# A gate stage in written order on four engines, with the rows of w_sp asked for two pairs ahead

## The chip, the cores and the metric

The kernel runs on one core of a Trainium2 chip. The time is the device time of one execution in microseconds; lower is better. Five engines work side by side, each through its own list of instructions in order: PE (matrix products, with PEld as its weight loads), ACT, DVE, POOL, and SP, which here only issues transfers. They wait for each other through semaphores. PE writes to PSUM, of which this stage uses four banks for its products; SBUF holds everything else.

## What is computed

One transformer block on x of 2048 x 512 in float32: attention with 32 heads, then a gated MLP whose gate mixes the rows of the sequence.

```python
h = x + _A_ref(_layernorm(x), A_wqkv, A_wo)           # attention, 32 heads of 16
z = _gelu(jnp.einsum("bsd,df->bsf", _layernorm(h), w_in))   # f = 1376
z1 = z[..., :Fh]                                      # Fh = 688
z2 = _layernorm(z[..., Fh:], axis=-1)
g = jnp.einsum("ts,bsf->btf", w_sp, z2) + b_sp[None, :, None]   # w_sp: 2048 x 2048
h2 = h + jnp.einsum("bsf,fd->bsd", z1 * g, w_out)
```

The change touches the product with `w_sp` and what follows it.

## The kernel before

The program has four parts: projections and attention; a stage that makes `z` (16 blocks of 128 rows); the gate stage; and a second pass that finishes the gate and multiplies by `w_out`. Every product is done as three products of float32r halves (`mm3`, lines 87 to 89: high x high, high x low, low x high), so an operand is first split: ACT copies the high half (L741, or L79 from PSUM), DVE subtracts it to get the low half (L742, or L84). `parts` and `split` do this, and `put` splits the two halves of a 128 x 1024 row of `w_sp` into a slot.

The product `w_sp @ z2` is 2 x 2 blocks times 2 x 2 blocks, done with seven block products in place of eight. A is `w_sp` (rows t and columns s, each in two halves), B is `z2` (s and f in two halves of 1024 and 344). The rows of A go in eight **pairs** p: rows p and p+8, in blocks of 128. For a pair, S1 = A21+A22, S2 = S1-A11, S3 = A11-A21, S4 = A12-S2. The B side (T1, T2, T3, N4) is made once, in the z stage.

- The **gate stage** (the loop at the head of the last `with`) computes for each pair g7 = S3 T3, g6 = S2 T2, g4 = A22 N4 and g5 = S1 T1, each of 8 blocks and 24 matmuls, and leaves three sums in `g_scr`: `p6` is a copy of g6 by ACT (L924), `p67` = g7+p6 (L925), `keep` adds these to g4 and g5 (L888) and stores them. S2 is stored in `s_scr`. While PE works on pair p, the operands of pair p+1 are loaded, combined and split: `rows_of_a` loads A11, A21 and A22 (six transfers of 256 KB, L747), forms S3, S1 and S2 on DVE (L761) and stores S2 (L776). Its tiles have the tags `xr` (three halves), `rc` and `o` (two halves each), so a tile of pair p+2 can be asked for only when the split of pair p+1 has read it. The split operands lie in seven slots that rotate (`old`, `now`, `new`). The products write to a pool of four banks, `ps_g`.
- Beside the last pair (`last`), the first needs of the second pass are made: A11, S4 and A12 of pair 0, the blocks of B (`b11`, one block per pair; `b22` and `b21`, eight blocks each, in the place of T3 and T2), read back from `z_scr` by `load_b` (L865) through two times three buffers, and `w_out` (`raw_u`, split to `wu`).
- The **second pass** computes for each pair g1 = A11 B11, g3 = S4 B22 and g2 = A12 B21, adds the stored sums (L1037, L1050, L1067) and the bias (L1038), multiplies by z1 (L1039 for the lower row of the pair, L1051 and L1068 for the upper), transposes (L1001), splits the transposes (`Out.turn`, L79 and L84), multiplies by `w_out` (`Out.multiply`) and adds h (`Out.store`, L1018). `fetch(p+1)` issues the loads for the next pair.

Order. In the second pass PE, ACT and DVE run in the order in which the code is written (`tc.manual_schedule`); SP there, and all engines in the gate stage, are ordered by a scheduler that has a model of each instruction's time and takes what it holds to be ready. Every engine then executes its list strictly in order. The pool tiles carry the waits: a tile is handed on when the last reader of its former content is done.

Of the kernel before, what the change touches and what calls it, by code (L numbers as in the profile page):

```python
# [18 lines left out]
P = 128  # L19
S = 2048  # L20
D = 512
# [23 lines left out]
def block_kernel(ctx: ExitStack, tc: tile.TileContext, x, wqkv, wo, w_in, w_sp4, b_sp, w_out, out):  # L45
# [717 lines left out]
    def rows_of_a(p, e):  # L763

        half = lambda name, tag: e2.tile([P, QB, P], F32, name=name, tag=tag, bufs=3 if tag == "xr" else 2)
        a11, a21, a22 = ([half(f"a{n}", tag) for _ in range(2)]
                         for n, tag in ((11, "xr"), (21, "rc"), (22, "o")))
        s3 = [e2.tile([P, QB, P], F32, name="s3", tag=f"o2{n}", bufs=1) for n in range(2)]
        load_a(a11, 0, 0, p)
        load_a(a21, 1, 0, p)  # L770
        load_a(a22, 1, 1, p)
        combine(e, s3, a11, a21, ALU.subtract)
        combine(e, a21, a21, a22, ALU.add)
        combine(e, a11, a21, a11, ALU.subtract)
        for n in range(2):
            nc.sync.dma_start(cut(s_scr[p])[n], a11[n])  # L776
        return {"s3": s3, "s2": a11, "a22": a22, "s1": a21}

    with ExitStack() as mid:
# [57 lines left out]
        for k in range(NB):  # L837
# [8 lines left out]
            if k == NB - 2:  # L846
                raw = rows_of_a(0, nc.vector)
                ops = {n: put(w[i], raw[n]) for i, n in enumerate(("s3", "s2", "a22"))}
# [3 lines left out]
    with ExitStack() as fin:  # L852
# [26 lines left out]
        ops["s1"] = put(f[0], raw["s1"])  # L879
        old, now = [None, None, f[1], f[2]], w + f[:1]  # L880
        for p in range(HB):
            nxt, new, last = {}, [old[2], old[3], now[0], now[1]], p + 1 == HB
            g7, g6, g4, g5 = [ps_g.tile([P, 512], F32, name="g")[:, :FC] for _ in range(4)]
# [7 lines left out]
            if not last:  # L891
                raw = rows_of_a(p + 1, nc.vector)
                nxt["s3"] = put(new[0], raw["s3"])
                nxt["s2"] = put(new[1], raw["s2"])
            else:
                t = [e2.tile([P, QB, P], F32, name="a11", tag="rc") for _ in range(2)]
                load_a(t, 0, 0, 0)
                a11 = put(f[0], t)
            put_b(b11, p, load_b(0, 0, p))
            if last:  # L900
                bs = [load_b(1, 1, k) for k in range(6)]

                raw_u = wc.tile([P, 4, D], F32, name="wr", tag="w2")
# [203 lines left out]
```

## Time and profile before

| | |
|---|---|
| times of three runs | 1907.54, 1910.86, 1911.50 us; median 1910.86 us |
| profiled execution | 1914.12 us; span of the core 1912.3 us, mean granted clock 0.994 |
| busy | PE 1883.8 us, DVE 1535.9, ACT 1328.8, POOL 203.9 |
| gate stage, pairs 0 to 7 | 1593.24 to 1713.80 us |
| pair 0 of the second pass | to 1749.73 us |
| pairs 1 to 7 and the end | to 1912.3 us |

How to read it: times are microseconds from the span's start. PE's busy time is counted from records whose ends are modelled, so what matters are PE's waits and its granted clock. A row of a timeline gives the start, the busy time of the (merged) instructions, engine, line, operation, output and input by the program's names with the buffer numbers left out, the shape and the count; in brackets the idle time just before and what ended it. Lines such as L742 belong to helpers that many places call; the names tell which. The line numbers are those of the kernel before.

### The profile page before, as it was taken

How to read it: one execution, taken by the hardware profiler on the slowest of the kernel's cores; microseconds unless marked ns; L12 is line 12 of the kernel's file. 1: busy time of each engine (PE TensorE's matmuls, PEld its weight loads, DVE VectorE, ACT ScalarE, POOL GpSimd, SP SyncE). 2: the span in 40 equal slices, each digit the busy share in tenths (PEclk: the TensorE clock that was granted, in tenths of full speed). 3: DMA queues.
4: the chain of work that ended last, by engine and by line, in shares of the span. 5: the costliest groups of instructions: out<-in, count | busy, mean ns of one | idle time of the engine just before them, and what ended most of it. 6: DMA issues, size and time to landing. Idle time of an engine off the chain costs nothing. (4 is left out here: it accounts for less than half of the span.)

```text
span 1912.3 us, 32432 instructions
## 1 busy us (share of the span) xinstructions
PE 1883.8 (99%) x11608; PEld 1068.5 (56%) x11608; DVE 1535.9 (80%) x3105; ACT 1328.8 (69%) x1733; POOL 203.9 (11%) x281
## 2 busy tenths in 40 slices
PE   9999999999999999999999999999999999997999
PEld 6765444444444444444444444444359989996887
DVE  6487999999999999999999999999537677665554
ACT  3335888888888888888888888888964345342221
POOL 2130000001011000000000000000015551001211
PEclk9999999999999999999999999999999999998999
DMA  5677111211221111111021021000045556657551
GB/s 189 183 199 182 40 24 31 71 25 28 49 51 32 38 34 21 37 39 24 19 50 33 13 49 31 22 13 5 7 107 161 154 172 203 191 185 237 181 180 34
DMA packets 148105, 159.82 MB, mean 84 GB/s; under 512 B 62952, under 2 KB 92664, under 8 KB 146408
## 3 DMA queue, kind: packets, MB, share of 16 engines
q1 hardware_dynamic: 143304, 146.48, 28.6%
q10 hardware_dynamic: 4608, 11.27, 1.5%
q8 instruction: 91, 1.49, 0.3%
q14 instruction: 70, 0.57, 0.1%
q0 software_dynamic: 32, 0.01, 0.0%
HBM read 101.16 MB, written 55.61 MB: 82 GB/s over the span
## 5 line engine op out<-in xcount | busy, mean ns | idle before, releaser
L611 ACT ACTIVATE pt<-s 128x1024 f32<-128x1024 f32 x1024 | 993.3, 1030 | 143.9 <-PE s L608 141.6
L208 DVE TENSOR_REDUCE mx<-m 128x1 f32<-128x512 f32 x1511 | 958.5, 683 | 104.9 <-PE m L203 61.6
L203 PE MATMUL m<-kst,qst 48*128 48x512 f32 x1511 | 606.3, 447 | 0.0
L619 PE MATMUL pv<-pt,vst 128*32 128x512 f32 x4096 | 550.9, 605 | 0.4 <-ACT o L626 0.4
L608 PE MATMUL s<-qst,kst 50*128 50x512 f32 x2048 | 465.6, 428 | 2.5 <-ACT pt L611 2.0
L203 PEld LDWEIGHTS m<-kst,qst 48*128 48x128 f32 x1511 | 262.9, 184 | 315.6 <-DVE mx L208 222.5
L608 PEld LDWEIGHTS s<-qst,kst 50*128 50x128 f32 x2048 | 222.8, 185 | 57.1 <-ACT pt L611 32.4
L203 PE MATMUL m<-uvs,qst 48*128 48x512 f32 x503 | 248.5, 495 | 0.0
L203 PEld LDWEIGHTS m<-uvs,qst 48*128 48x128 f32 x503 | 91.8, 183 | 207.2 <-DVE mx L208 205.3
L217 DVE CUSTOM_DVE_ANT_0 ab<-m,ab 128x512 f32<-128x512 f32 x252 | 171.5, 681 | 3.8 <-ACT ab L213 2.0
L619 PEld LDWEIGHTS pv<-pt,vst 128*32 128x32 f32 x4096 | 82.9, 108 | 161.0 <-issue 154.9
L213 ACT ACTIVATE ab<-m 128x512 f32<-128x512 f32 x251 | 151.2, 602 | 16.7 <-PE tp L203 10.5
L81 POOL CAST mparts<-nm 128x16 fp32r<-128x16 f32 x32 | 6.3, 196 | 910.9 <-DVE nm L223 910.9
L741 ACT ACTIVATE ws<-a 128x512 fp32r<-128x512 f32 x80 | 46.6, 624 | 66.0 <-issue 26.7
L87 PE MATMUL acc<-wi,hT 128*128 128x344 f32 x256 | 82.9, 324 | 0.0
L88 PE MATMUL acc<-wi,hT 128*128 128x344 f32 x256 | 81.8, 319 | 0.0
L89 PE MATMUL acc<-wi,hT 128*128 128x344 f32 x256 | 81.8, 319 | 0.0
L742 DVE TENSOR_TENSOR ws<-a,ws 128x512 fp32r<-128x512 f32 x80 | 56.0, 743 | 19.5 <-ACT ws L741 19.5
L87 PE MATMUL g<-b,ws 128*128 128x344 f32 x192 | 65.7, 342 | 2.7 <-ACT p L924 2.7
L79 ACT ACTIVATE pT<-tp 128x384 fp32r<-128x384 f32 (+2 forms) x48 | 18.3, 382 | 66.7 <-PE tp L1001 49.2
L88 PE MATMUL g<-b,ws 128*128 128x344 f32 x192 | 62.5, 326 | 0.0
L89 PE MATMUL g<-b,ws 128*128 128x344 f32 x192 | 62.4, 325 | 0.0
(188 smaller groups left out, 2176.4 us busy)
## 6 DMA issues: line engine op xcount, KB each, us to landing
a<-in_w_sp SPq DMA_DIRECT2D x80, 256.0 KB
qst<-q_scr SPq DMA_DIRECT2D x192, 64.0 KB
kst<-k_scr SPq DMA_DIRECT2D x48, 256.0 KB
z_scr<-z ACTq DMA_DIRECT2D x32, 344.0 KB
k_scr<-part SPq DMA_DIRECT2D x16, 512.0 KB
q_scr<-part SPq DMA_DIRECT2D x16, 512.0 KB
z<-z_scr SPq DMA_DIRECT2D x14, 344.0 KB
b<-z_scr SPq DMA_DIRECT2D x24, 172.0 KB
```

Of the source, the lines that this page charges most:

```text
L87: nc.tensor.matmul(ps, lh, rh, start=first, stop=False)
L88: nc.tensor.matmul(ps, lh, rl, start=False, stop=False)
L89: nc.tensor.matmul(ps, ll, rh, start=False, stop=last)
L203: nc.tensor.matmul(acc, q[r, p, c], keys[r, p], start=True, stop=True)
L208: nc.vector.reduce_max(at(t, e if t else e - 1), acc, axis=AX.X)
L213: nc.scalar.activation(ab[0], acc, AF.Abs)
L217: nc.vector.tensor_tensor_reduce(ab[0], acc, ab[0], 0.5, LOW, ALU.add, ALU.max, at(0, 0))
L608: nc.tensor.matmul(s[:, t, :], k[r, p, kb * P:(kb + 1) * P], q[r, p, :], start=True, stop=True)
L611: nc.scalar.activation(t, s, AF.Exp, scale=DH ** -0.5)
L619: nc.tensor.matmul(pv[0][32 * j:32 * j + 32, :], vst[hg % 2][:, c:c + 32], pts[j % 2][:, j // 2, :], start=kb == 0, stop=kb == NB - 1)
L741: nc.scalar.activation(hi, src, AF.Copy)
L742: (nc.gpsimd if el == "pool" else nc.vector).tensor_sub(lo, src, hi.bitcast(F32))
```

## The change

The arithmetic stays. The gate stage is put into `manual_schedule` for PE, ACT, DVE and SP, and the second pass is now inside the same block, so that SP runs in written order there too. `rows_of_a` is taken apart into `ask` (loads), `difference` (S3) and `sums` (S1, S2 and the store of S2), and the loads for pair p+2 are written into pair p, each behind the split that frees its buffers: A22 and A11 behind A22's split, A21 behind S1's. Within a pair S3 is now split before the sums, and `b` is asked one pair ahead. The copy `p6` stands in the code behind the split of the next pair's A22, as it did before.

In pair 6 the places of the loads that no longer have a pair are taken by A12, S2 and A11 of the second pass's pair 0 and by six blocks of `b22`; in pair 7 every split of a block asks for the next one (`put_next`). `w_out` is asked behind the last blocks of `b22`, and all its splits stand after the last `keep`. The first load of stored sums is asked behind the second `keep`. In the second pass `fetch` asks A11, S2 and A12 first, `h` is asked for the present pair, and in pair 0 the splits for pair 1 stand behind the transposes and, for A11, ahead of the first multiplication.

```diff
@@ -760,21 +760,27 @@
-    def rows_of_a(p, e):
-        half = lambda name, tag: e2.tile([P, QB, P], F32, name=name, tag=tag, bufs=3 if tag == "xr" else 2)
-        a11, a21, a22 = ([half(f"a{n}", tag) for _ in range(2)]
-                         for n, tag in ((11, "xr"), (21, "rc"), (22, "o")))
+    def half(name, tag, bufs=2):
+        return [e2.tile([P, QB, P], F32, name=name, tag=tag, bufs=bufs) for _ in range(2)]
+    def ask(i, j, p, tag):
+        t = half(f"a{i}{j}", tag, 3 if tag == "xr" else 2)
+        load_a(t, i, j, p)
+        return t
+    def difference(a11, a21):
         s3 = [e2.tile([P, QB, P], F32, name="s3", tag=f"o2{n}", bufs=1) for n in range(2)]
-        load_a(a11, 0, 0, p)
-        load_a(a21, 1, 0, p)
-        load_a(a22, 1, 1, p)
-        combine(e, s3, a11, a21, ALU.subtract)
-        combine(e, a21, a21, a22, ALU.add)
-        combine(e, a11, a21, a11, ALU.subtract)
+        combine(nc.vector, s3, a11, a21, ALU.subtract)
+        return s3
+    def sums(p, a11, a21, a22):
+        combine(nc.vector, a21, a21, a22, ALU.add)
+        combine(nc.vector, a11, a21, a11, ALU.subtract)
         for n in range(2):
             nc.sync.dma_start(cut(s_scr[p])[n], a11[n])
-        return {"s3": s3, "s2": a11, "a22": a22, "s1": a21}
@@ -844,8 +850,10 @@
             if k == NB - 2:
-                raw = rows_of_a(0, nc.vector)
-                ops = {n: put(w[i], raw[n]) for i, n in enumerate(("s3", "s2", "a22"))}
+                a11, a21, a22 = ask(0, 0, 0, "xr"), ask(1, 0, 0, "rc"), ask(1, 1, 0, "o")
+                s3 = difference(a11, a21)
+                sums(0, a11, a21, a22)
+                ops = {n: put(w[i], t) for i, (n, t) in enumerate((("s3", s3), ("s2", a11), ("a22", a22)))}
     early.close()
@@ -860,10 +868,13 @@
         def load_b(i, j, k):
-            t = (f1.tile([P, FC], F32, name="b", bufs=3) if k % 2 else
+            staged[0] += 1
+            t = (f1.tile([P, FC], F32, name="b", bufs=3) if staged[0] % 2 else
                  e2.tile([P, FC], F32, name="b", tag="hn", bufs=3))
             nc.sync.dma_start(t, z_scr[1][(HB * i + k) * P:(HB * i + k + 1) * P, j * FC:(j + 1) * FC])
             return t
+        staged = [0]
@@ -876,10 +887,14 @@
         f = [Slot(fs, f"f{i}") for i in range(3)]
-        ops["s1"] = put(f[0], raw["s1"])
+        ops["s1"] = put(f[0], a21)
         old, now = [None, None, f[1], f[2]], w + f[:1]
+        order = fin.enter_context(tc.manual_schedule(engines={E.PE, E.Activation, E.DVE, E.SP}))
+        a11, a21, a22 = ask(0, 0, 1, "xr"), ask(1, 0, 1, "rc"), ask(1, 1, 1, "o")
+        b = load_b(0, 0, 0)
         for p in range(HB):
             nxt, new, last = {}, [old[2], old[3], now[0], now[1]], p + 1 == HB
+            ahead = p + 2 if p + 2 < HB else None
             g7, g6, g4, g5 = [ps_g.tile([P, 512], F32, name="g")[:, :FC] for _ in range(4)]
@@ -889,20 +904,12 @@
             if not last:
-                raw = rows_of_a(p + 1, nc.vector)
-                nxt["s3"] = put(new[0], raw["s3"])
-                nxt["s2"] = put(new[1], raw["s2"])
+                nxt["s3"] = put(new[0], difference(a11, a21))
+                sums(p + 1, a11, a21, a22)
+                nxt["s2"] = put(new[1], a11)
             else:
-                t = [e2.tile([P, QB, P], F32, name="a11", tag="rc") for _ in range(2)]
-                load_a(t, 0, 0, 0)
-                a11 = put(f[0], t)
-            put_b(b11, p, load_b(0, 0, p))
-            if last:
-                bs = [load_b(1, 1, k) for k in range(6)]
-                raw_u = wc.tile([P, 4, D], F32, name="wr", tag="w2")
-                nc.sync.dma_start(raw_u, w_out[:4 * P, :].rearrange("(a p) c -> p a c", p=P))
-                raw_u = [raw_u[:, :2, :], raw_u[:, 2:, :]]
+                a11 = put(f[0], a11)
+            put_b(b11, p, b)
             if p:
                 product(g7, ops["s3"], T["t3"])
             else:
@@ -910,80 +917,107 @@
                     product(g7, ops["s3"], T["t3"], blocks)
                     product(g6, ops["s2"], T["t2"], blocks)
             if not last:
-                nxt["a22"] = put(new[2], raw["a22"])
+                nxt["a22"] = put(new[2], a22)
+                a22 = ask(1, 1, ahead, "o") if ahead else ask(0, 1, 0, "o")
+                if ahead:
+                    s2, a11 = a11, ask(0, 0, ahead, "xr")
+                else:
+                    s2 = half("s4", "xr", 3)
+                    for n in range(2):
+                        nc.sync.dma_start(s2[n], cut(s_scr[0])[n])
             else:
                 b22 = [zc.tile([P, HB, FC], F32R, name="b22", tag=f"t3_{i}") for i in range(2)]
-                for k in range(HB):
-                    put_b(b22, k, bs[k] if k < len(bs) else load_b(1, 1, k))
-                s4raw = [e2.tile([P, QB, P], F32, name="s4", tag="xr", bufs=3) for _ in range(2)]
-                for n in range(2):
-                    nc.sync.dma_start(s4raw[n], cut(s_scr[0])[n])
+                b21 = []
+                asked = [(1, 1, k) for k in range(6, HB)] + [(1, 0, k) for k in range(HB)]
+                def put_next(b, k):
+                    put_b(b, k, bs.pop(0))
+                    if asked:
+                        bs.append(load_b(*asked.pop(0)))
+                for k in range(6):
+                    put_next(b22, k)
+                combine(nc.vector, s2, a22, s2, ALU.subtract)
+                s4 = put(f[1], s2)
+                for k in range(6, HB):
+                    put_next(b22, k)
+                raw_u = wc.tile([P, 4, D], F32, name="wr", tag="w2")
+                nc.sync.dma_start(raw_u, w_out[:4 * P, :].rearrange("(a p) c -> p a c", p=P))
+                raw_u = [raw_u[:, :2, :], raw_u[:, 2:, :]]
             if p:
                 product(g6, ops["s2"], T["t2"])
             nc.scalar.activation(p6, g6, AF.Copy)
             nc.vector.tensor_add(p67, g7, p6)
             if not last:
-                nxt["s1"] = put(new[3], raw["s1"])
+                nxt["s1"] = put(new[3], a21)
+                if ahead:
+                    a21 = ask(1, 0, ahead, "rc")
+                else:
+                    a11 = ask(0, 0, 0, "rc")
+                b = load_b(0, 0, p + 1)
+                if not ahead:
+                    bs = [load_b(1, 1, k) for k in range(6)]
             else:
-                t = [e2.tile([P, QB, P], F32, name="a12", tag="o") for _ in range(2)]
-                load_a(t, 0, 1, 0)
-                combine(nc.vector, s4raw, t, s4raw, ALU.subtract)
-                s4 = put(f[1], s4raw)
-                a12 = put(f[2], t)
+                a12 = put(f[2], a22)
                 b21 = [zc.tile([P, HB, FC], F32R, name="b21", tag=f"t2_{i}") for i in range(2)]
                 for k in range(HB):
-                    put_b(b21, k, load_b(1, 0, k))
-            product(g4, ops["a22"], T["n4"])
-            keep(1, g4, p67)
-            if last:
+                    put_next(b21, k)
                 for f0, n in FB[4:]:
                     t = e2.tile([P, D], F32, name="wr", tag="rc")
                     nc.sync.dma_start(t[:n], w_out[f0:f0 + n, :])
                     raw_u.append(t[:n])
-                parts(wu[0][:, :2, :], wu[1][:, :2, :], raw_u[0])
+            product(g4, ops["a22"], T["n4"])
+            keep(1, g4, p67)
             product(g5, ops["s1"], T["t1"])
             keep(2, g5, p67)
+            if last:
+                t = zc.tile([P, HB * FC], F32, name="qz", tag="t1_1")
+                first = (t[:, :3 * FC].rearrange("p (i c) -> p i c", c=FC),
+                         [t[:, (3 + 2 * i) * FC:(5 + 2 * i) * FC] for i in range(2)])
+                nc.sync.dma_start(first[0], g_scr[0].rearrange("i p c -> p i c"))
             keep(0, g5, p6)
             ops, old, now = nxt, now, new
+        for i in (1, 0):
+            nc.sync.dma_start(first[1][i], z_scr[0][HB * i * P:(HB * i + 1) * P, :])
...
+        for i, places in enumerate([[w[:, 2 * i:2 * i + 2, :] for w in wu] for i in range(2)]
+                                   + [[w[:, 4, :] for w in wu], [t[:fn, j * D:(j + 1) * D] for j in range(2)]]):
+            parts(*places, raw_u[i])
...
+        rows = lambda p, i: slice((p + HB * i) * P, (p + HB * i + 1) * P)
         def fetch(p):
-            q, z1 = first if not p else (f2.tile([P, 3, FC], F32, name="q"),
...
+            raw = [half("a11"), half("a12"), half("s2")]
+            load_a(raw[0], 0, 0, p)
+            for n in range(2):
+                nc.sync.dma_start(raw[2][n], cut(s_scr[p])[n])
+            load_a(raw[1], 0, 1, p)
+            z1 = [f2.tile([P, FH], F32, name=f"z1{i}") for i in range(2)]
+            q = f2.tile([P, 3, FC], F32, name="q")
             nc.sync.dma_start(q, g_scr[p].rearrange("i p c -> p i c"))
             for i in (1, 0):
-                nc.sync.dma_start(z1[i], z_scr[0][rows[i], :])
-            raw = None
-            if p:
-                raw = [half("a11"), half("a12"), half("s2")]
-                load_a(raw[0], 0, 0, p)
-                load_a(raw[1], 0, 1, p)
-                for n in range(2):
-                    nc.sync.dma_start(raw[2][n], cut(s_scr[p])[n])
+                nc.sync.dma_start(z1[i], z_scr[0][rows(p, i), :])
+            return q, raw, z1
+        def fetch_h(p):
             h = [f2.tile([P, D], F32, name=f"h{i}") for i in range(2)]
             for i in (1, 0):
-                nc.sync.dma_start(h[i], h_scr[rows[i], :])
-            return q, raw, z1, h
+                nc.sync.dma_start(h[i], h_scr[rows(p, i), :])
+            return h
@@ -1018,63 +1052,67 @@
-        prev, nxt = None, fetch(0)
-        with tc.manual_schedule(engines={E.PE, E.Activation, E.DVE}):
-            for p in range(HB):
-                (q, _, z1, h), last = nxt, p + 1 == HB
-                nxt = None if last else fetch(p + 1)
...
+        prev, nxt = None, (first[0], None, first[1])
+        for p in range(HB):
+            (q, _, z1), last = nxt, p + 1 == HB
+            nxt = None if last else fetch(p + 1)
+            h = fetch_h(p)
...
+            if p and not last:
+                a11 = put(f[0], nxt[1][0])
...
+            if p and not last:
+                combine(nc.vector, nxt[1][2], nxt[1][1], nxt[1][2], ALU.subtract)
+                s4 = put(f[1], nxt[1][2])
...
+            if not p:
+                a11 = put(f[0], nxt[1][0])
+                bot.multiply(range(len(FB)))
+            nc.vector.tensor_add(left, g2, left)
+            (nc.vector if last else nc.gpsimd).tensor_mul(left, left, z1[0][:, :FC])
+            if not p:
+                combine(nc.vector, nxt[1][2], nxt[1][1], nxt[1][2], ALU.subtract)
+                s4 = put(f[1], nxt[1][2])
+            if not last:
+                a12 = put(f[2], nxt[1][1])
```

More of the change, by code (lines that the diff above doesn't have):

```diff
@@ L959, in block_kernel @@
-        t = zc.tile([P, HB * FC], F32, name="qz", tag="t1_1")
-        first = (t[:, :3 * FC].rearrange("p (i c) -> p i c", c=FC),
-                 [t[:, (3 + 2 * i) * FC:(5 + 2 * i) * FC] for i in range(2)])
         late.close()
         f2 = fin.enter_context(tc.tile_pool(name="fin_2", bufs=2))
+        rows = lambda p, i: slice((p + HB * i) * P, (p + HB * i + 1) * P)
         def fetch(p):
-            rows = [slice((p + HB * i) * P, (p + HB * i + 1) * P) for i in range(2)]
             half = lambda n: [f2.tile([P, QB, P], F32, name=n) for _ in range(2)]
-            q, z1 = first if not p else (f2.tile([P, 3, FC], F32, name="q"),
-                                         [f2.tile([P, FH], F32, name=f"z1{i}") for i in range(2)])
+            raw = [half("a11"), half("a12"), half("s2")]
[5 more added lines that the diff above has]
+            q = f2.tile([P, 3, FC], F32, name="q")
@@ L1081 @@
+        prev.multiply(range(3, 6), False)
+        prev.turn((0, 3))
+        prev.multiply(range(3))
+        prev.store()
 def kernel(**inputs):
```

97 lines of the change are left out of this document (39 added, 58 removed).

## The prediction

> **What bounds the kernel now.** I read the page first, then busy time by stretches, the timeline of each engine around the two seams of the gate stage, and the queue of SP. The page gives the span and shows one dip:
>
> ```profile
> span 1912.3 us, 32432 instructions
> ...
> PE   9999999999999999999999999999999999997999
> ...
> PEclk9999999999999999999999999999999999998999
> ```
>
> PE is the bound almost everywhere; only slice 37 (1721 to 1769 us) has both an idle PE and a reduced clock. Cutting the end of the program at product boundaries shows how much (length, then busy us and count for PE, PEld, DVE, ACT, POOL, then clock, DMA share, GB/s):
>
> ```profile
> 1608.37:1623.40 15.03, 15.03 (x98) 15.03 (x97) 12.41 (x23) 5.33 (x10) 0.00 (x0) 1.00 0.73 225
> 1668.60:1683.60 15.00, 15.00 (x98) 14.94 (x97) 9.89 (x18) 4.96 (x9) 0.00 (x0) 1.00 0.51 170
> 1713.80:1749.73 35.93, 22.30 (x99) 19.50 (x97) 20.97 (x37) 13.27 (x27) 2.81 (x2) 0.76 0.80 267
> 1773.50:1795.28 21.78, 21.78 (x123) 19.00 (x121) 12.50 (x22) 6.19 (x13) 4.47 (x3) 1.00 0.58 178
> ```
>
> A pair of the gate stage and a pair of the second pass are pure PE time (15.03 and 21.78 us, clock 1.00). The stretch between them, pair 0 of the second pass, takes 35.93 us at a clock of 0.76. PE's timeline there has three waits:
>
> ```profile
> 1710.04 0.32 PE L87 MATMUL g<-t,ws 128*128 128x344 f32 x1
> 1716.68 0.53 PE L87 MATMUL g<-b,ws 128*128 128x344 f32 x1 [2.71 <-ACT p L924]
> 1729.92 0.98 PE L1001 MATMUL tp<-ident,pr 128*128 128x128 f32 x6 [2.01 <-ACT pr L1038]
> 1743.11 0.80 PE L87 MATMUL acc<-wu,pT 128*128 128x512 f32 x1 [8.90 <-ACT pT L79]
> 1749.73 0.43 PE L87 MATMUL g<-b,ws 128*128 128x344 f32 x1
> ```
>
> Why they exist is on ACT, which works strictly in its order:
>
> ```profile
> 1715.79 0.49 ACT L741 ACTIVATE b<-b 128x344 fp32r<-128x344 f32 x1 [5.24 <-DMA b<-z_scr]
> 1716.18 0.44 ACT L924 ACTIVATE p<-g 128x344 f32<-128x344 f32 x1
> ...
> 1737.43 1.24 ACT L741 ACTIVATE ws<-a 128x512 fp32r<-128x512 f32 x2 [7.82 <-DMA a<-in_w_sp]
> ```
>
> The copy that frees PE a PSUM bank (L924) stood behind a split of `b` whose load had not landed, and the split of the transposes (L79) stood behind the split of `a11` for the next pair, whose load landed at 1737.4. The middle wait is named ACT, but the DVE product L1039 (start 1728.94, 0.88 us) ended at 1729.82, just before.
>
> After each wait the clock halves for a while (us stretches of 2):
>
> ```profile
> 1716.00:1718.00 2.00, 1.32 (x5) 1.32 (x6) 1.48 (x4) 2.00 (x6) 0.00 (x0) 0.71 0.48 156
> 1718.00:1720.00 2.00, 2.00 (x9) 2.00 (x8) 2.00 (x5) 2.00 (x7) 0.00 (x0) 0.50 0.55 158
> 1720.00:1722.00 2.00, 2.00 (x14) 2.00 (x13) 2.00 (x6) 2.00 (x3) 0.00 (x0) 0.94 0.57 175
> ```
>
> **The change, part by part.** *Counts.* Written out, the changed kernel has the same number of instructions on every engine, the same number of DMAs, and PE's sequence is the same instruction by instruction. So nothing is added or removed; only orders on ACT, DVE and SP change.
>
> *The seam to the second pass: removed waits.* Without waits, pair 0 of the second pass needs 72 matmuls of the gate kind at 15.03/96 = 0.157 us (11.28), six transposes (1751.72 to 1752.30, 0.58) and 18 multiplications (1754.27 to 1758.74, 4.47): 16.33 us. It took 35.93, so 19.6 us are there to win: 13.62 of waits and 5.98 of half clock. The new order takes each cause away. The 24 `b` blocks are asked from pair 6 on in a chain of six buffers, and p6 stands on ACT behind b22 alone; `a11` of pair 1 is put after the splits of pair 0's transposes. What is late next, counted on DVE from pair 7's start T with the pitches of the rows (0.605 for 128x512, 0.43 for 128x344): two keeps, a11, b11 to T+2.5; b22 must wait for g7's end (T+3.76, it takes T3's place); six of b22, the S4 combine, its split with one hop over ACT, two more, p67, a12, eight of b21 to T+15.4; three keeps to 16.7; the four splits of w_out (1.14, 1.14, 0.6, 0.6) to 20.2; three L1037 (1.5) and L1039 (0.88) to 22.6. PE reaches the transposes at T+15.03+60x0.157 = T+24.4. Slack 1.8 us, from which the last two b21, queued on SP behind the 1 MB of w_out, may take up to 1.5. The q load follows the second keep's store on SP (T+16.5); before, it was asked at 1722.18 and used at 1727.44, so at most 5.3 us: T+21.8, against 20.2 at which DVE asks for it; that too eats the slack, not more. The a11 of pair 1 is asked when the w_out splits free the memory (T+20.2); before, 1729.79 to 1737.43, 7.6 us: T+27.9, split by T+30, needed at T+31.4. I cost the seam at 0 (bounds 0 and 5: one wait of up to 3 and its clock).
>
> *The first seam: a new wait.* ps_g has four banks. Pair 1's g7 needs one of pair 0's back, and the first free one is g6's, freed by the copy p6. Before, the scheduler put p6 of pair 0 early:
>
> ```profile
> 1602.08 0.43 ACT L924 ACTIVATE p<-g 128x344 f32<-128x344 f32 x1
> ...
> 1603.52 0.69 DVE L761 TENSOR_TENSOR s<-a,a 128x512 f32<-128x512 f32 x1 [0.80 <-DMA a<-in_w_sp]
> 1604.40 0.69 DVE L761 TENSOR_TENSOR s<-a,a 128x512 f32<-128x512 f32 x1 [0.19 <-DMA a<-in_w_sp]
> 1605.01 2.49 DVE L761 TENSOR_TENSOR a<-a,a 128x512 f32<-128x512 f32 x4
> 1607.41 1.29 DVE L742 TENSOR_TENSOR ws<-s,ws 128x512 fp32r<-128x512 f32 x2
> ```
>
> In written order p6 of pair 0 stands on ACT behind all splits of pair 1's S3, S2, b and A22, and these wait for pair 1's a21, whose buffer only comes free after S1 of pair 0 (asked 1599.84, landed 1603.5 and 1604.4). Then: differences to 1605.0, S3's lower halves to 1606.3, four sums to 1608.7, then on ACT S2's second half 0.52, b 0.41, A22 2x0.52, p6 0.43: 1611.1. PE wants the bank at 1608.37, where it began without a wait before. So 2.7 us of waiting. Bounds: 2 (if the loads land half a microsecond earlier) and 4.5 (a22 is now queued behind a21: 0.5 MB more at the 213 to 325 GB/s of that stretch). The clock: the waits of 2.71 and 2.01 us were followed by 11.23 us for 60 matmuls worth 9.4, and by 4.29 us for work worth 2.45: 1.83 us each. The new wait is as long, so I add 1.8. The Trainium skill (TensorE: Matmul & The Clock Gate, Part 1) says that the array goes to half clock after at least one idle window of about 3.4 us; by that a wait of 2.7 us would keep the clock, and the sum would be -16.9. The trace does not agree: 2.01 us of idle were enough.
>
> *The steady gate pairs: 0.* DVE's own loop is: differences, splits, sums, splits to S1 (14 of 0.605, two of 0.43, a hop: 9.6 us), then the a21 load; from S1 done to the next difference it took 4.2 to 5.5 us before (1655.4 to 1659.62, 1669.5 to 1675.03), with all six loads issued in a bunch. Now a22 and a11 go out some 2 us ahead of a21, so I take 4.2: 13.8, under 15.03, and the loop keeps up. In pair 1 it starts late: from the sums (1608.7) S2, b, A22, p67 and S1 bring DVE to 1613.4, the next a21 lands at 1617.6, p6 of pair 1 comes 7.5 later at 1625.1, and g7 of pair 2 wants its bank at 1627.9 (1611.1, 15.03 and 1.8 of clock). Slack 2.8 us, growing by about 1 a pair. The cover is gone if a load takes 2.8 us longer.
>
> *SP in written order.* Behind each ask stand the stores of s_scr and q. The waiting asks are those whose buffer DVE frees late; nobody waits soon for the stores (q has two buffers). In the second pass pair p+1's loads go out some 3 us before pair p starts, its h a little later; PE has no wait there now and gets none: 0.
>
> *Sum.* -19.6 + 2.7 + 1.8 = -15.1 us. The profiled execution took 1914.12 us (span 1912.3 and 1.8 around it): it would be 1899.0. It lies 3.3 above the median of the three runs, 1910.86; from that I forecast 1895.8.
>
> **Rivals.**
> A second wait stays (at the pass-2 transposes, at pair 1's a11, or at g7 of pair 2): the slacks of 0.2 to 2.8 us are thin, and loads behind w_out took 5.24 us of ACT's time before. Price 1 to 3 us and 1.8 of clock: 1898.6 to 1900.6, two of them 1904.
> The new wait costs less: the clock stays up through an idle stretch as short as 2.7 us (the row after 2.01 us is against it), 1910.86-19.6+2.7 = 1894.0, or the loads land early enough that no wait is left, 1891.3. The Trainium skill's section named above states the first.
> Slower: the w_sp loads land late in every gate pair. Before, a late load only delayed DVE, because the scheduler put p6 ahead of the splits that wait for it; now p6 stands behind A22's split and holds a bank. If a21 lands L after its ask, DVE's loop takes 9.6+L; over 5.4 each microsecond of L makes each pair longer, and each wait adds 1.8 of clock. With L = 8 (nearest row: the 7.6 to 1737.43, in a stretch with a DMA share of 0.80, where gate pairs have 0.51 to 0.73) the first pair eats the slack and five lose 2.6+1.8, 22 us: 1917.8. It decides at L of about 7, where four to five pairs lose 3.4. The 4.2 to 5.5 of the gate pairs speak against it.
> No change to be measured: the second pass's loads only move later on SP, so that the waits at the transposes and at a11 come back whole (2.0+1.8 and 8.9+2.2): -0.2, 1910.7. Against it: pass 2's first blocks are all asked before pair 7 ends.
>
> **How the numbers follow.** Forecast (one new wait at pair 1, clean second seam) 0.50, its own range 1894.5 to 1898.5; second wait 0.22; cheaper 0.12; no change 0.06; slower 0.10. Leaving out the last two and the outer edge gives 1890.5 to 1904. A measurement tells about 0.2% (3.8 us) here from no change: faster 0.84 (the first three), same 0.06, slower 0.10.
>
> **What would show it.** Right: PE's timeline has one wait near 1608.4 of 2 to 4.5 us released by ACT's copy p<-g, then 15.03 a pair; the stretch from g5 of pair 7 to pair 1 of the second pass is 16 to 18 us at clock near 1; DVE's first L1037-like step comes before PE reaches the transposes. Wrong: no wait at pair 1 (then the bank came from elsewhere), waits of PE on ACT's p<-g in several pairs (the slower rival), or a wait at pT that names a11's load again.

## The result, and the profile after

The changed kernel took 1915.36 us (median of 8) beside 1911.18 us of the kernel before (median of 8): a ratio of 1.0023, 95% interval [1.0012, 1.0034]. In a second comparison it took 1911.98 beside 1909.79 us: 1.0009 [1.0001, 1.0018]. It is slower by one or two tenths of a per cent; the forecast was 1895.8 us.

The page of its profiled execution (1915.18 us) still has the dip in slice 37, now at 8 tenths of PE where it was 7:

```profile
span 1913.1 us, 32433 instructions
...
PE   9999999999999999999999999999999999998999
...
PEclk9999999999999999999999999999999999998999
```

Busy time by stretches, first the gate stage, then pair 0 of the second pass, called the seam below (length, then busy us and count of PE, PEld, DVE, ACT, POOL, clock, DMA share, GB/s):

```profile
1595.86:1721.47 125.61, 122.04 (x768) 120.26 (x768) 86.12 (x152) 44.91 (x86) 0.00 (x0) 1.00 0.57 184
1721.47:1750.58 29.11, 19.38 (x99) 17.13 (x97) 20.31 (x37) 13.06 (x27) 2.22 (x2) 0.82 0.80 267
```

The gate stage was 120.56 us before and is 125.6; the seam was 35.93 and is 29.1, where 16.3 was forecast. From pair 1 of the second pass on nothing changed (158.4 us from the start of its first product to that of the last in both). PE's timeline shows where the two stretches lose time:

```profile
1612.81 0.43 PE L87 MATMUL g<-t,ws 128*128 128x344 f32 x1 [1.65 <-ACT p L952]
...
1643.90 0.43 PE L87 MATMUL g<-t,ws 128*128 128x344 f32 x1 [0.48 <-ACT p L952]
1659.93 0.42 PE L87 MATMUL g<-t,ws 128*128 128x344 f32 x1 [0.70 <-ACT p L952]
...
1706.33 0.42 PE L87 MATMUL g<-t,ws 128*128 128x344 f32 x1 [0.44 <-ACT p L952]
1723.31 0.42 PE L87 MATMUL g<-b,ws 128*128 128x344 f32 x1 [1.68 <-ACT p L952]
1733.98 0.39 PE L87 MATMUL g<-b,ws 128*128 128x344 f32 x1 [2.90 <-DVE q L903]
1742.04 1.51 PE L1035 MATMUL tp<-ident,pr 128*128 128x128 f32 x6 [5.16 <-DVE pr L1073]
```

The wait of 8.90 us on the transposes' split is gone. In its place PE waits for p6 at the head of most gate pairs, then for p6 again at the second pass's first product (1.68 us, where the first profile of before had 2.71), for g2's bank and for the second pass's first product with z. What stands behind p6 is the DVE's own round, here the one that runs in pair 3 (of 0 to 7) and prepares pair 4:

```profile
1652.00 1.36 DVE L761 TENSOR_TENSOR s<-a,a 128x512 f32<-128x512 f32 x2 [4.57 <-DMA a<-in_w_sp]
1653.47 1.29 DVE L742 TENSOR_TENSOR ws<-s,ws 128x512 fp32r<-128x512 f32 x2
1654.68 2.49 DVE L761 TENSOR_TENSOR a<-a,a 128x512 f32<-128x512 f32 x4
1657.63 1.29 DVE L742 TENSOR_TENSOR ws<-a,ws 128x512 fp32r<-128x512 f32 x2 [0.46 <-ACT ws L741]
1658.84 0.51 DVE L742 TENSOR_TENSOR b<-b,b 128x344 fp32r<-128x344 f32 x1
1659.27 1.29 DVE L742 TENSOR_TENSOR ws<-a,ws 128x512 fp32r<-128x512 f32 x2
1660.47 0.51 DVE L953 TENSOR_TENSOR p<-g,p 128x344 f32<-128x344 f32 x1
1660.90 1.28 DVE L742 TENSOR_TENSOR ws<-a,ws 128x512 fp32r<-128x512 f32 x2
...
1667.20 1.46 DVE L761 TENSOR_TENSOR s<-a,a 128x512 f32<-128x512 f32 x2 [3.75 <-DMA a<-in_w_sp]
```

and on SP's queue the requests that belong to it:

```profile
1659.98 2.83 SPq L747 DMA_DIRECT2D a<-in_w_sp  x6
```

From one difference to the next pass 15.20 us: 10.2 to the end of S1's split, then 5.0 until the next A11 and A21 are there. All six loads, named "two pairs ahead" in the code, leave within 2.83 us, and the first of them 8.0 us after the difference. A21's buffers come free only with S1's split, the last of the round; A22's come free one split earlier; and A11's two requests (1660.96 and 1661.48), whose buffers S2's split has left by 1658.9, stand behind A22's on SP.

The same round in the kernel before, DVE's timeline and then SP's:

```profile
1645.51 0.69 DVE L761 TENSOR_TENSOR s<-a,a 128x512 f32<-128x512 f32 x1 [3.43 <-DMA a<-in_w_sp]
...
1659.62 0.69 DVE L761 TENSOR_TENSOR s<-a,a 128x512 f32<-128x512 f32 x1 [3.76 <-DMA a<-in_w_sp]
```

```profile
1652.02 3.76 SPq L747 DMA_DIRECT2D a<-in_w_sp  x6
```

There the first request leaves 6.5 us after the difference, and the next difference follows it by 7.6 us, against 7.2 here. In the last four of the six rounds, two profiles of each kernel, the first part is 5.6 to 6.5 us before and 7.7 to 8.0 in the changed kernel, the second 6.8 to 8.9 and 7.2 to 8.2. So what the written order made longer is the way to the first request; from there the loads take as long as they did.

Over six rounds the mean is 15.72 us (first difference 1604.35, seventh 1698.67), while PE needs 14.9 to 15.03 a pair.

### The profile page after: what moved, and what is told of

Read it like the earlier page. It is cut to its first block, busy times and chain, and to the rows that moved or that the text cites. A ratio compares the mean times of both kernels' runs of the same rounds, so it can differ in the third digit from the quotient of the medians.

```text
span 1913.1 us, 32433 instructions
## 1 busy us (share of the span) xinstructions
PE 1881.7 (98%) x11608; PEld 1066.5 (56%) x11608; DVE 1536.7 (80%) x3105; ACT 1328.8 (69%) x1733; POOL 203.1 (11%) x281
## 4 chain that ended last, share of the span: by engine, by line
PE 83%; DMA 6%; DVE 6%; ACT 2%; issue 1%; SPq 1%; ACTq 0%; POOL 0%; DVEq 0%; POOLq 0%
PE pv L619 26%; PE m L203 25%; PE s L608 12%; PE acc L87 5%; PE acc L89 4%; PE acc L88 4%; DMA a<-in_w_sp 2%; DMA h_scr<-xr 2%; PE g L87 2%; PE g L89 1%; PE g L88 1%; DVE ws L742 1%; ACT ws L741 1%; DMA o<-o_scr 1%; PE tp L1035 1%
## 5 line engine op out<-in xcount | busy, mean ns | idle before, releaser
L87 PE MATMUL g<-b,ws 128*128 128x344 f32 x192 | 65.2, 340 | 4.6 <-DVE q L903 2.9
L87 PE MATMUL g<-t,ws 128*128 128x344 f32 x192 | 62.0, 323 | 4.2 <-ACT p L952 3.6
L741 ACT ACTIVATE ws<-s 128x512 fp32r<-128x512 f32 x32 | 19.3, 630 | 63.7 <-DVE s L761 63.6
```

Source lines behind the costliest of these rows:

```text
L87: nc.tensor.matmul(ps, lh, rh, start=first, stop=False)
L741: nc.scalar.activation(hi, src, AF.Copy)
```

## The experiments

The theories: (1) written order puts p6 behind splits that wait, and this holds PE's bank; (2) the queue within the seam, above all w_out's 1 MB ahead of the last b21 blocks, makes what is left of the seam; (3) the DVE's round through loads and buffers is longer than a pair, and the seam ends a fixed time after the last difference; and, as the rival of all, that two single profiles differ by chance.

**Both kernels once more.**

> The changed kernel once more. If the two profiles stand for their kernels, the gate stage (first gate product to the second pass's first product) is again about 125.6 us and the way from there to pair 1 of the second pass about 29.0 us, and what lay 2.6 us later before the stage was a difference between executions that does not come back. If the difference between the two profiles is chance, these stretches vary by 2 us or more from one execution to the next. The time is 1915.4 us either way.

Measured 1911.98 us; gate stage 124.6, seam 30.6, round 15.54 us, and the 2.6 us before the stage did not come back.

> The kernel before once more. If its first profile stands for it, the gate stage is 120.4 us and the way from the second pass's first product to pair 1 about 36 us again, 156.5 together. If the seam of before varies (its three waits hang on when loads land), the two together lie 2 us or more from that, and the comparison of the two first profiles said too little.

Measured 1911.92 us in its one run. Busy time by stretches of this second profile of the kernel before, gate stage and seam:

```profile
1594.71:1715.10 120.39, 120.39 (x768) 120.39 (x769) 87.40 (x160) 47.03 (x91) 0.00 (x0) 1.00 0.62 198
1715.10:1747.27 32.17, 19.79 (x98) 17.34 (x96) 20.40 (x36) 12.09 (x25) 2.82 (x2) 0.79 0.80 261
```

Its seam is 32.2 us, not 35.9: the wait of 2.71 us at the first product did not occur. The two stretches together are 152.6 us here and 156.5 in the first profile, against 154.7 and 155.3 in the changed kernel. So the seam of the kernel before is not one number, and its first profile had the longer one of the two. Against the second profile the change lost 4.3 to 5.2 us in the gate stage and won 1.5 to 3.1 in the seam, a net loss of 2.1 to 2.7 us, where the medians say 2.2 and 4.2.

**The bank alone.**

```diff
-            g7, g6, g4, g5 = [ps_g.tile([P, 512], F32, name="g")[:, :FC] for _ in range(4)]
+            g7, g4, g5 = [ps_g.tile([P, 512], F32, name="g")[:, :FC] for _ in range(3)]
+            g6 = ps_o.tile([P, 512], F32, name="acc")[:, :FC]
```

> g6 of every gate pair lies in a PSUM bank of the output products, idle in this stage, and not in the ring of four; nothing else is changed. Theory 1a (the gate stage lost 5.0 us because ACT's copy p6, written behind the splits of A22, holds the bank that the next pair's first product needs): the six waits on p6 go, pairs come back to 15.03 us and the stage to about 121 us; with the 1.68 us at the second pass's first product the time is about 1908 to 1909. Theory 1b (DVE's loop of difference, splits, request and landing, 15.7 us, paces the stage, and the bank is only where it shows): the waits move to the split of S3, pairs stay at 15.5 to 15.8 us after the first slack is used up, and the time is 1912 to 1914.

Measured 1911.01 us, 1.0004 [0.9995, 1.0013]. Busy time of gate stage and seam, then PE's waits in its timeline:

```profile
1592.66:1713.04 120.38, 120.38 (x769) 120.38 (x769) 81.70 (x144) 41.94 (x81) 0.00 (x0) 1.00 0.56 182
1713.04:1747.60 34.56, 23.38 (x98) 21.12 (x96) 25.20 (x47) 16.76 (x35) 2.22 (x2) 0.75 0.81 264
```

```profile
1720.79 0.65 PE L87 MATMUL g<-b,ws 128*128 128x344 f32 x1 [3.83 <-DVE p L954]
1730.09 0.62 PE L87 MATMUL g<-b,ws 128*128 128x344 f32 x1 [2.79 <-DVE q L904]
1738.16 1.51 PE L1036 MATMUL tp<-ident,pr 128*128 128x128 f32 x6 [4.57 <-DVE pr L1074]
```

Both forecasts missed in place. The gate stage came back whole, as theory 1 said, but the seam took the gain: together 154.9 us, as in the changed kernel. The DVE's round stayed at 15.74 us. PE ran ahead on its slack and waited in the seam for what the same round delivers. The p6 waits were where the loss showed, not its cause: without them the time is not told apart from the changed kernel's beside it (1911.98).

**Written order only from the last pair on.** The scheduler orders the first seven pairs; requests and code are those of the changed kernel.

```diff
-        order = fin.enter_context(tc.manual_schedule(engines={E.PE, E.Activation, E.DVE, E.SP}))
...
+            if last:
+                order = fin.enter_context(tc.manual_schedule(engines={E.PE, E.Activation, E.DVE, E.SP}))
```

> The written order begins only with the last gate pair; the first seven pairs are left to the scheduler as in the kernel before, with the requests and the code of the changed kernel. Theory 1 (the written order of the gate pairs costs 5.0 us): the stage is back at 120 to 122 us and the seam keeps its gain, so about 1909 to 1911. Rival (the requests two pairs ahead, not the order, make the loads late): the stage stays at 125 us and the time at 1915. Rival (the scheduler puts the last pair's loads behind other work): the seam gives back the 7 us, 1915 or more.

Measured 1906.90 us, 0.9982 [0.9972, 0.9991], faster than both kernels. The round is 14.76 us and the seam 25.0 us at a clock of 0.93. The gate stage has 124.1 us, but for another reason than in the changed kernel: one wait of 1.87 us for a bank freed by a late addition, with 3.4 us at half clock behind it. The gain came from the seam, not from the gate stage as I had forecast: with a shorter round the last blocks are there earlier.

**The queue within the seam, w_out later.**

```diff
-                raw_u = wc.tile([P, 4, D], F32, name="wr", tag="w2")
-                nc.sync.dma_start(raw_u, w_out[:4 * P, :]...)
...
                 for k in range(HB):
                     put_next(b21, k)
+                raw_u = wc.tile([P, 4, D], F32, name="wr", tag="w2")
+                nc.sync.dma_start(raw_u, w_out[:4 * P, :]...)
```

> The request for four fifths of w_out (1 MB) moves behind the requests for the last two blocks of b21. Theory 2 (the wait of 2.90 us for g2's bank and most of the 5.16 us before the transposes come from these two blocks landing behind w_out): the last b21 block is split 3 us earlier, the first wait goes and the second falls by 1 to 3 us, 1910 to 1912. Rival (the splits of w_out, now later, hold the DVE in front of the second pass's first additions): the 5.16 us stay or grow, 1914 to 1917.

Measured 1912.79 us, 1.0015 [1.0006, 1.0024]: between the two forecasts, and not told apart from the changed kernel beside it (1911.98). The mechanism is the rival's: the wait before the transposes grew from 5.16 to 7.12 us. The DVE's timeline shows the last b21 blocks with hardly a wait, and then w_out's splits:

```profile
1727.74 1.05 DVE L742 TENSOR_TENSOR b<-b,b 128x344 fp32r<-128x344 f32 x2 [0.67 <-ACT b L741]
1728.71 1.35 DVE L903 TENSOR_TENSOR q<-g,p 128x344 f32<-128x344 f32 x3
1734.64 3.56 DVE L742 TENSOR_TENSOR wu<-wr,wu 128x1024 fp32r<-128x1024 f32 x4 [4.58 <-ACT wu L741]
1738.31 1.54 DVE L1071 SCALAR_TENSOR_TENSOR pr<-g,bias,qz 128x344 f32<-128x344 f32 x3
```

The wait for g2's bank went, and a wait of 4.58 us before w_out's splits took its place: these are written ahead of the second pass's first additions (L1071), so whatever lands last holds them.

**The queue within the seam, additions first.**

```diff
                 a12 = put(f[2], a22)
+                product(g4, ...); product(g5, ...)
+                for i, (g, other) in enumerate(((g5, p6), (g4, p67), (g5, p67))):
+                    nc.vector.tensor_add(q[i], g, other)
+                ... nc.sync.dma_start(first[0], g_scr[0]...)
                 b21 = ...
```

> The changed kernel; in the last gate pair the three additions that free the gate products' banks and the request for the first q go ahead of the splits of b21. Theory 4 (in the seam the DVE works off a queue behind the last b21 block: additions, splits of w_out, then the wait for q): the wait for g2's bank goes, the splits of w_out start 1.3 us earlier, the first additions of the second pass need not wait for q, and pair 1 of the second pass starts 2.5 to 3 us earlier: seam 26 to 28 us, 1909 to 1910 where the changed kernel has 1912. Rival (w_out's landing sets the end): the splits of w_out wait instead and nothing is gained, 1912.

Measured 1913.95 us, 1.0013 [1.0004, 1.0022]: nothing gained. The wait for g2's bank went and the additions of L1071's kind (L1078 here) no longer waited for q, but the splits of b21 that free the last two buffers now stand behind the three additions (1.36 us), the last requests behind these splits, and ACT waited 6.63 us for the blocks instead of 4.90. PE has one wait of 8.52 us before the transposes, and the seam 29.8 us.

**The round shortened.** In every pair but the last, the splits of S2 and S1, which free A11's and A21's buffers, come right behind the sums, each with its request; S3, b and A22 follow. With g6 in the other bank.

```diff
-                nxt["s3"] = put(new[0], difference(a11, a21))
+                s3 = difference(a11, a21)
                 sums(p + 1, a11, a21, a22)
                 nxt["s2"] = put(new[1], a11)
+                s2, a11 = a11, ask(0, 0, ahead, "xr")
...
+                nxt["s1"] = put(new[3], a21)
+                a21 = ask(1, 0, ahead, "rc")
+                nxt["s3"] = put(new[0], s3)
+                put_b(b11, p, b)
                 nxt["a22"] = put(new[2], a22)
                 a22 = ask(1, 1, ahead, "o") if ahead else ask(0, 1, 0, "o")
```

> As the run with g6 in another bank, and in each gate pair but the last the splits of S2 and S1, whose buffers the next A11 and A21 need, come right behind the sums, each with its request behind it, and the splits of S3, b and A22 (with A22's request) after them. Theory 3 (DVE's loop from one difference over splits, requests and landing to the next sets when the last pair's blocks are asked for, and the seam ends some 52 us after the last difference): the loop falls from 15.7 to the pair's 14.9 us, the last difference comes 4 to 6 us earlier after the stage's start than the 102.9 us of the run with the bank alone, the gate stage stays at 120.3 us, the seam falls from 34.7 to about 30 us, and the time is 1905 to 1907. Rival (the way back from a request is what is long, and six loads asked apart land as late as six asked together): the last difference moves by less than 2 us, 1909 to 1911. Rival (S1's split waits for g6's product on ACT and DVE and holds S3's): waits appear at the first gate product of the pairs, 1912 or more.

Measured 1901.11 us, 0.9951 [0.9939, 0.9964]. DVE's timeline in a gate pair, and gate stage and seam by stretches:

```profile
1639.23 1.28 DVE L761 TENSOR_TENSOR s<-a,a 128x512 f32<-128x512 f32 x2
1640.43 2.50 DVE L761 TENSOR_TENSOR a<-a,a 128x512 f32<-128x512 f32 x4
1643.09 1.29 DVE L742 TENSOR_TENSOR ws<-a,ws 128x512 fp32r<-128x512 f32 x2 [0.16 <-ACT ws L741]
1646.62 1.29 DVE L742 TENSOR_TENSOR ws<-a,ws 128x512 fp32r<-128x512 f32 x2 [2.24 <-ACT ws L741]
...
1654.27 1.28 DVE L761 TENSOR_TENSOR s<-a,a 128x512 f32<-128x512 f32 x2
```

```profile
1592.27:1713.35 121.08, 120.68 (x768) 120.37 (x769) 92.53 (x165) 49.22 (x98) 0.00 (x0) 1.00 0.68 203
1713.35:1736.76 23.41, 18.63 (x99) 16.96 (x97) 14.60 (x25) 8.31 (x15) 2.23 (x2) 0.85 0.81 272
```

The first request leaves 4.1 to 5.8 us after the difference, and the difference no longer waits for a load; the round shown is as long as PE's pair (15.04 us; 13.92 over six rounds, since the first ones are shorter). The last difference starts 92.1 us after the stage's start, 10.8 us earlier than with the bank alone, and the seam loses 11.2 us. The edit moves splits and requests together; no run moves the requests alone, so how much of this is SP's order and how much the DVE's stays open.

> The shortened loop (splits of S2 and S1 with their requests right behind the sums) without the other bank: g6 stays in the ring of four, and p6 is copied on ACT right behind S1's split. Theory 3 (the loop is what the changed kernel lost): as fast as with the other bank, 1900 to 1903, gate stage 120.3 to 121.5 us. Rival (the bank is needed as well): waits on p6 come back at the first product of the pairs and the time is 1905 or more.

The same order with g6 in the ring of four: 1901.32 us, 0.9966 [0.9952, 0.9979], round 13.99 us, gate stage 121.6, seam 23.3. It is not told apart from the run with the other bank: with p6 copied right behind S1's split, the bank is not needed.

**The round lengthened.**

```diff
-                nxt["s3"] = put(new[0], difference(a11, a21))
+                s3 = difference(a11, a21)
+                combine(nc.vector, s3, a11, a21, ALU.subtract)
+                nxt["s3"] = put(new[0], s3)
```

> The kernel with g6 in another bank (1911.0 us, loop 15.74 us), and the difference for S3 is computed twice in a row, 1.29 us more on the DVE in each of the seven loops; nothing else waits for it. Theory 3: loop 17.0 us, last difference 7.7 us later, its own second computation 1.3 us more, the end 9 us later: about 1920. Rival (the landing of the loads paces the loop and the DVE has room before it): the second computation is hidden and the time stays within 2 us of 1911.

Measured 1921.35 us, 1.0064 [1.0052, 1.0077]: by the medians 10.3 us more than with the bank alone (11.2 if each is taken against the kernel before beside it, 12.4 and 1.2) for 9.0 us of added DVE work, where 9 was expected. The round is 17.04 us; PE now waits for S3's split in the gate stage (129.0 us) and the seam stays at 34.5. PE's timeline of the first two of these waits:

```profile
1656.11 0.42 PE L87 MATMUL g<-t,ws 128*128 128x344 f32 x1 [1.39 <-ACT ws L741]
1673.53 0.43 PE L87 MATMUL g<-t,ws 128*128 128x344 f32 x1 [1.25 <-ACT ws L741]
```

**What is left of the seam.** On top of the shortened round:

> Both edits of the two runs above in one kernel. If the loop and the seam's queue are links of one chain, the gains add up: 1902 to 1904. If one takes the other's place (w_out's or the last blocks' landing is the bound), it is no faster than the better of the two.

1903.00 us, 0.9957 [0.9944, 0.9969]; the seam fell to 19.5 us in its profile, but the time is not told apart from that of the run without the early additions.

> Shortened loop, other bank, early additions, and the first two blocks of b21 are split ahead of those additions, so that the requests for b21's last two blocks no longer wait for them. If those two blocks' landing (5.0 us waited for on ACT in the run with both edits) sets the start of w_out's splits and with it the seam, the last split comes 2 us earlier and the seam is 17.5 to 18.5 us instead of 19.7: 1898 to 1901. If w_out's 1 MB ahead of them sets it, nothing changes: 1901 to 1903.

1899.89 us, 0.9954 [0.9941, 0.9966], the lowest median of all, seam 19.0 us at a clock of 1.00. The requests went out 4.0 us earlier, but the blocks, behind w_out, were there only 0.8 us earlier (both counted from the stage's start), and the wait before the transposes fell from 2.88 to 2.41 us. The time is not told apart from that of the shortened round alone.

> As the run with the shortened loop, the other bank, the early additions and b21's first blocks ahead of them (1899.9 us, seam 19.2 us); in addition the splits of w_out (3.6 us on the DVE) stand behind the second pass's first additions and their product with z, which pair 0 now makes in place of q. If w_out's splits, placed ahead of these additions, are what is left of the seam's wait (2.4 us before the transposes, and the half clock after it), the wait goes and pair 1 starts 2.5 to 4.5 us earlier: seam 15 to 17 us, 1895.5 to 1898. Rival (the additions wait for b21's last blocks or for q and z anyway, or the splits, now later, hold the multiply of pair 0): 1899 to 1902.

1902.82 us, 0.9959 [0.9944, 0.9974]: no gain. The wait before the transposes fell to 0.77 us, but 1.27 us came at the multiply of pair 0 (seam 19.1), and pair 1's loads, whose memory w_out's splits free, went out 4.5 us later; from pair 1 on PE needed 161.3 us instead of 158.4.

Together (round: mean from difference to difference; stage and seam in us, from one profile each; where two values stand, the first comparison or profile and the second):

| kernel | median us | ratio to before | round | stage | seam |
|---|---|---|---|---|---|
| before, median and one later run | 1911.18, 1911.92 | 1 | 14.29, 13.97 | 120.6, 120.4 | 35.9, 32.2 |
| changed, twice | 1915.36, 1911.98 | 1.0023, 1.0009 | 15.72, 15.54 | 125.6, 124.6 | 29.1, 30.6 |
| other bank | 1911.01 | 1.0004 | 15.74 | 120.4 | 34.6 |
| order from the last pair on | 1906.90 | 0.9982 | 14.76 | 124.1 | 25.0 |
| shortened round, other bank | 1901.11 | 0.9951 | 13.92 | 121.1 | 23.4 |
| shortened round alone | 1901.32 | 0.9966 | 13.99 | 121.6 | 23.3 |
| other bank, lengthened round | 1921.35 | 1.0064 | 17.04 | 129.0 | 34.5 |

Nine profiles are of kernels whose last pair is in written order, without the three runs on what is left of the seam. In them the second pass's first additions start 39.8 to 41.7 us after the last difference, whether that comes 92.1 us after the stage's start (shortened round) or 110.6 (lengthened). That is theory 3. Theory 1 named the place where it shows. Theory 2 can hold only for what is left once the round is short: there the seam of single profiles fell from 23.4 to 19.0 us, but no gain in time could be told apart.

## Why the prediction was wrong

*What bounds the kernel: right in place, wrong in size.* The seam was the place, but the 35.93 us were those of one execution. The second profile had 32.2. I then went from that execution's forecast (1899.0) to the median by taking off 3.3 us more. The excess of that execution lay, as far as one more profile can tell, in the very seam whose waits I had already taken off (3.8 us longer than in the second profile). So up to 3.3 us were counted twice.

*The first seam: +2.7 and +1.8 of clock.* The wait came where the prediction put it, on p6 of pair 0, at 1.65 and 1.31 us (bounds 2 to 4.5), and the clock stayed at 1.00 behind it. The term was mis-sized, 4.5 us for 1.3 to 1.7: both halves of A21 had landed 10.0 us after the stage's start (1605.84 in a stage from 1595.86), and I had counted with the 11.2 us of the kernel before (1604.40 in one from 1593.24).

*The steady gate pairs: 0. This step failed.* I put the round at 9.6 us of DVE work and 4.2 of landing, 13.8 us, from the argument that A22 and A11 leave some 2 us ahead of A21. A22 does (1659.98 against 1661.95), A11 only by 1.0 us, and it was no gain on the kernel before: there, where I took the loads to leave in a bunch, the first left 2.8 us ahead of the fifth and 6.5 us after the difference, and in written order it leaves 7.7 us or more after it. Measured, as means of six rounds in two profiles: 10.1 us to the end of S1's split and 5.5 to 5.6 from there (single rounds 5.0 to 6.0), together 15.5 to 15.7 us. The slack that was to grow by 1 us a pair shrank by 0.5 to 0.7. The changed kernel lost 4.2 to 5.2 us in the stage, the first wait included. This is the mechanism of the rival "slower", with p6 and the bank as it described them, and the sign that the prediction named for it came: PE waits on ACT's p<-g in several pairs. It came at a landing of 5.5 us instead of the 7 from which I let it decide. Its price in the stage was far too high: the waits behind the first were under 0.8 us and no half clock followed them, so they cost some 3 us where I had put 22. The rest of what the long round cost was paid in the seam.

*The seam: 0 above 16.3. This step failed most, by 12.8 to 14.3 us.* The count on the DVE began with A11 of the second pass split by T+2.5, with T the start of pair 7. Here are ACT's timeline and the DVE's for it (T is 1706.33):

```profile
1714.39 1.26 ACT L741 ACTIVATE ws<-a 128x512 fp32r<-128x512 f32 x2 [7.06 <-DMA a<-in_w_sp]
...
1731.68 0.49 ACT L741 ACTIVATE b<-b 128x344 fp32r<-128x344 f32 x1 [4.90 <-DMA b<-z_scr]
```

```profile
1715.05 1.32 DVE L742 TENSOR_TENSOR ws<-a,ws 128x512 fp32r<-128x512 f32 x2 [5.20 <-ACT ws L741]
...
1732.20 0.52 DVE L742 TENSOR_TENSOR b<-b,b 128x344 fp32r<-128x344 f32 x1 [4.22 <-ACT b L741]
...
1733.33 1.35 DVE L903 TENSOR_TENSOR q<-g,p 128x344 f32<-128x344 f32 x3
1734.60 3.54 DVE L742 TENSOR_TENSOR wu<-wr,wu 128x1024 fp32r<-128x1024 f32 x4
1739.61 1.54 DVE L1071 SCALAR_TENSOR_TENSOR pr<-g,bias,qz 128x344 f32<-128x344 f32 x3 [1.47 <-DMA g_scr<-q]
```

A11's split starts at T+8.1, because its buffers are A21's and its request closes pair 6's late round. The DVE waits 5.20 us for it. The last b21 blocks cost ACT a wait of 4.90 us behind w_out and the DVE 4.22, where I allowed 1.5; q cost 1.47. So L1071 starts at T+33.3 instead of T+20.2, and these three waits are 10.9 of the 13.1 us. The first of these terms is shown by the shortened and the lengthened round. The others interlock: moving w_out, the additions or w_out's splits alone each put another wait in the place of the one removed, and only on top of the shortened round did the seam fall to 19 us.

*SP in written order: 0.* Right for the second pass. In the gate stage I looked for who waits for the stores, not for which request stands in front of another: A11's left 2.0 us after S2's split was done with their buffers, because A22's stood ahead of them. By the rows this is part of the later first request; no run tells its share.

*The clock.* After a wait of 2.01 us and one of 2.71 in the first profile I charged 1.8 us for any wait of that size. Over all runs the limit is not sharp. Half clock for 3.4 us followed waits of 1.38 us (lengthened round), 1.87 (order from the last pair on) and 1.89 (second profile of the changed kernel). None followed others of 1.25, 1.39, 1.55, 1.65, 1.68 and 2.29 us, nor those of 2.41 and 2.88 us in two runs with early additions, whose seam has a clock of 1.00. The Trainium skill (TensorE: Matmul & The Clock Gate, Part 1) speaks of a free-running window of about 3.4 us, and the length of the half-clock stretches agrees with it. That at least one idle window of this length is needed, as the same part states, does not agree with the waits of 1.38 to 1.89 us. What decides between waits of 1.4 and 2.9 us stays open here.

## What to carry to other kernels

Where an order is written by hand, follow each staging buffer round its whole loop (use, last split, request, landing, next use) and compare that with the bounding engine's period; the split that frees the buffer the next round needs first belongs first, and its request ahead of requests that still wait. A loop that is 0.7 us a round too long (15.72 against 15.03 us) can stay hidden behind slack and be paid in one sum at the next stage, so removing the wait that shows it (here a PSUM bank) only moves it. Before going from one profiled execution to the median, find out in which stretch that execution is long: if it is the stretch that the change removes, the excess must not be taken off twice.

## What the runs showed beside this

The seam of the kernel before differed by 3.8 us between two executions, and the start of the gate stage lay between 1591.6 and 1595.9 us in the profiles of these kernels, although PE's products up to there are the same. A difference of 2 us between two single profiles of this kernel says nothing. Stretches measured from their own start say more, but the seam shows that one of them can vary by more than that as well. Six w_sp loads of 256 KB, requested within 2.8 us, needed 7.2 us from the first request to the difference that uses them (1659.98 to 1667.20), about 218 GB/s worked out from these, beside a load of b and the stores of s_scr and q.
